# Block attention and FFN in one kernel: transposes and narrow attn*v products placed between the FFN's 512-column products

## Chip, cores and metric

The kernel runs on one core of a Trainium2 chip. The metric is the device time of one execution in microseconds (us); the median of several executions is compared.

## The reference

Two stages, all in float32. First a block-causal attention over q, k, v of shape (8 batches, 8 heads, 576 positions, 64), then a feed-forward network (FFN) on the 4608 tokens with 512 features that come out of it:

```python
scores = scale * np.matmul(q, k.transpose(0, 1, 3, 2))
mask = block_i >= block_j                      # blocks of 64 positions
scores = np.where(mask, scores, -1000000000.0)
scores = scores - np.max(scores, axis=-1, keepdims=True)
attn = np.exp(scores)
attn = attn / (np.sum(attn, axis=-1, keepdims=True) + 1e-09)
...
x = np.ascontiguousarray(attn_out.transpose(0, 2, 1, 3)).reshape(B * S, H * D)
h = x @ w_in                                   # 512 -> 2048
g = np.where(pos, h, np.where(neg, 0.0, (h + beta) ** 2 / (4.0 * beta)))
return (g @ w_out).astype(np.float32)          # 2048 -> 512
```

## The kernel before

**Precision.** Products run on the type float32r. To keep float32's accuracy, an operand is split into a high word and a low word (`hi`, and `lo`, the remainder), and a product is made of two or three partial products.

**Attention.** The work goes by pairs of heads: 8 batches of 4 pairs, 32 pairs (`Pair`, with `b` the batch and `hp` the pair). One pair goes through `scores` (two accumulated products into a PSUM bank, row maximum on VectorE, exp on ScalarE, reciprocal and scaling on VectorE, L497 to L520), three groups of query tiles for each of the two heads (`scores(j, g)`) and the last 64 queries of both heads together (`scores_last`). The probabilities lie with queries on partitions and must be turned: they go through a DMA into a float32r tile (`prr`, L251), and `turn(j, g)` and `turn_last` transpose them on TensorE, 128 columns at a time (L559), into a PSUM bank, from which `split` (L552, L554) writes hi and lo words to the tiles `pa` and `pb`. `attn_v_first` and `attn_v` multiply them with v (`weighted`, L598): products of 320, 256, 192, 128 and 64 columns. `add_words` (L620, L621) adds the two words' sums and `store_x` writes x for the FFN.

**q and k.** For batches 0 and 1 they are split and then transposed. From batch 2 on (`raw`) they are transposed as they are (`turned_raw`, L403, four transposes for a head into one bank; `turned_last`, L444, one transpose for the last blocks) and split by four operations out of PSUM (`parted`, L390, L391, L396, L397). This is done for the next pair while the present one is worked on; `turned_last` is done in the pair itself.

**Batches 2 and later** (`far`) have one more property: a pair's last transpositions and its attn*v run on into the steps of the next pair, in which it is called `old`.

**FFN.** For each of 9 chunks of 512 tokens and each of 16 slices of 128 hidden features, `ffn_in` makes 12 products of 512 columns into the one bank `ph` (L777), the activation and the split follow on ScalarE, VectorE and GpSimd (L786 to L792), and `ffn_out` makes 12 products of 512 columns into the four banks `po` (L801, L806).

**PSUM.** Eight banks: four for `po`, one for `ph`, three "work" banks, which all scores, transpositions and attn*v take in turn (`work_bank`).

**Order of the work.** `attention_steps` is a generator that yields eight times for a pair. After each yield from step 36 on, the loop at the end (L845) emits one block of 12 FFN products. So in the program TensorE gets an attention part, in one piece, then 12 wide products, and so on. A scheduler then orders each engine's instructions; it keeps to the order of the program except where, by its own estimate, an instruction isn't ready and a later one is. In the part with batches 2 and later TensorE's order in the trace is that of the program. One pair of heads is then, on TensorE (T transposes of probabilities, Q transposes of q and k, S scores, A attn*v, F an FFN product; the group or the head in brackets):

```
step 0   T x3 (1,1 of old), S x4 (0,0), A x8 (first, of old), F x12
step 1   T x4 (1,2 of old), S x2 (0,1), Q x1 (last blocks), F x12
step 2   A x10 (head 1 of old), S x2 (0,2), F x12
step 3   T x3 (0,0), S x8 (last queries), F x12
step 4   T x3 (0,1), S x4 (1,0), Q x4 (head 0 of next), F x12
step 5   T x4 (0,2), S x2 (1,1), F x12
step 6   T x5 (last queries), S x2 (1,2), F x12
step 7   T x3 (1,0), A x10 (head 0), Q x4 (head 1 of next), F x12
```

Of the kernel before, what the change touches and what calls it, by code (L numbers as in the profile page):

```python
# [23 lines left out]
def block_attn_then_ffn(  # L24
# [53 lines left out]
    def work_bank(name):  # L78
# [178 lines left out]
    class Pair:  # L257
# [141 lines left out]
        def turned_raw(self, j):  # L399

            ps = work_bank("ps_qk")
            for t in range(NTL):
                nc.tensor.transpose(  # L403
                    ps[:, t * P : (t + 1) * P].bitcast(F32R), self.qk[:, j * NTL + t, :, :], ident_r
                )
            self.parted(
                lambda x: x[:, j, :SM].rearrange("p (c t) -> p c t", t=NTL),
                ps[:, :SM].rearrange("p (t c) -> p c t", t=NTL),
            )
            for a, bt, hi0 in ((qa, qb, 0), (ka, kb, D)):  # L410
                nc.sync.dma_start(
                    a[:D, j, :SM].bitcast(F32), bt[hi0 : hi0 + D, j, :SM].bitcast(F32)
                )

        def turned(self, is_q, j):
# [7 lines left out]
            for t in range(NTL):  # L423
                nc.tensor.transpose(
                    ps[:, t * P : (t + 1) * P].bitcast(F32R), src[:, j * NTL + t, :, :], ident_r
                )

# [11 lines left out]
        def turned_last(self):  # L439

            ps = work_bank("ps_qk")
            if self.raw:
                ps = ps[:, :P]
                nc.tensor.transpose(ps.bitcast(F32R), self.qk[:, 2 * NTL, :, :], ident_r)  # L444
                ps = ps.rearrange("p (h c) -> p h c", h=2)
                self.parted(last_blocks, ps)
                for i, a in enumerate((qa, ka)):
                    nc.vector.tensor_scalar_mul(
                        last_blocks(a)[:D], ps[i * D : (i + 1) * D], 1.0 if i else SCALE
                    )  # L450
                return
            for i, src in enumerate((self.qs, self.ks)):
                nc.tensor.transpose(
                    ps[:, i * P : (i + 1) * P].bitcast(F32R), src[:, 2 * NTL, :, :], ident_r
                )
            for i, (a, bt, hi0) in enumerate(((qa, qb, 0), (ka, kb, D))):
# [26 lines left out]
        def product(self, ps, j, c0, k0, n, first, last):  # L483
            nc.tensor.matmul(  # L484
                ps, qa[:KA, j, c0 : c0 + P], ka[:KA, j, k0 : k0 + n], start=first, stop=False
            )
            nc.tensor.matmul(  # L487
                ps, qb[:, j, c0 : c0 + P], kb[:, j, k0 : k0 + n], start=False, stop=last
            )

# [65 lines left out]
        def transposed(self, out, parts, c0, n):  # L556
            src = parts[c0 // TCH][:, c0 % TCH : c0 % TCH + n] if self.hop else parts[0][:, c0 : c0 + n]
            if self.hop:
                nc.tensor.transpose(out.bitcast(F32R), src, ident_r)  # L559
            else:  # L560
                nc.tensor.transpose(out, src, ident)  # L561

# [31 lines left out]
        def weighted(self, ps, j, parts, first=True, last=True):  # L594
            for i, (kt, lo_col, mov) in enumerate(parts):
                vt = self.vs[j][: (BLK if self.plain and kt == NTL else P), kt, :, :]
                for m, x in enumerate(mov):
                    nc.tensor.matmul(  # L598
                        ps[:, lo_col:], vt, x,
                        start=first and i == 0 and m == 0,  # L600
                        stop=last and i == len(parts) - 1 and m == len(mov) - 1,
                    )

# [66 lines left out]
    def attention_steps():  # L670
# [10 lines left out]
        for i, cur in enumerate(pairs + [None]):  # L681
            nxt = pairs[i + 1] if i + 1 < len(pairs) else None
            far = old is not None and old.far
            near = old is not None and not old.far
            if far:
                old.turn(1, 1)
            if cur:
# [22 lines left out]
            if not cur:  # L710
                return
            if cur.far:
                cur.scores(0, 2)
            else:
                cur.begin()
                cur.scores(0, 2)
                cur.turn(0, 0)
            yield
            if cur.far:
                cur.begin()  # L720
                cur.turn(0, 0)
                cur.scores_last()
            else:
                cur.scores_last()
                cur.turn(0, 1)
            if nxt:
                nxt.load_qk()
                nxt.split_q()
            yield
            if nxt:  # L730
                nxt.split_k()
            if cur.far:
                cur.turn(0, 1)
                cur.scores(1, 0)
            else:
                cur.scores(1, 0)
                cur.turn(0, 2)
            if nxt:
                nxt.turned(True, 0)
            yield  # L740
            if cur.far:
                cur.turn(0, 2)
                cur.scores(1, 1)
            else:
                cur.scores(1, 1)
                cur.turn_last()
            if nxt:
                nxt.turned(False, 0)
            yield
            if cur.far:  # L750
                cur.turn_last()
                cur.scores(1, 2)
            else:
                cur.scores(1, 2)
                cur.attn_v(0)
                cur.turn(1, 0)
            yield
            if cur.far:
                cur.turn(1, 0)
                cur.attn_v(0)  # L760
# [3 lines left out]
            if nxt:  # L764
                nxt.turned(True, 1)
            yield
            old = cur


    def ffn_in(c, fc):  # L770
# [4 lines left out]
        for cc in range(NCC):  # L775
            for i, (w, x) in enumerate(((wih, xh), (wih, xl), (wil, xh))):
                nc.tensor.matmul(  # L777
                    ph, w[:, cc, fs], x[:, cc, xs],
                    start=(cc == 0 and i == 0), stop=(cc == NCC - 1 and i == 2),
                )  # L780

# [15 lines left out]
    def ffn_out(po, c, fc, gh, gl, wo):  # L797
        for tt in range(NTT):
            ts_ = slice(tt * P, (tt + 1) * P)
            for w in range(2):  # L800
                nc.tensor.matmul(  # L801
                    po[tt], gh[:, ts_], wo[:, w, :], start=(fc == 0 and w == 0), stop=False
                )
        for tt in range(NTT):
            ts_ = slice(tt * P, (tt + 1) * P)
            nc.tensor.matmul(po[tt], gl[:, ts_], wo[:, 0, :], start=False, stop=fc == NFC - 1)  # L806
        if fc < NFC - 1:
# [12 lines left out]
    def feed_forward():  # L820
        prev = None
        for c in range(NCH):
            for fc in range(NFC):
                cur = (c, fc, *ffn_in(c, fc))
                yield
                if prev is not None:
                    if prev[1] == 0:
                        po = [ps_o.tile([P, DM], F32, tag="po", name="po") for _ in range(NTT)]
                    ffn_out(po, *prev)
                    yield  # L830
                prev = cur
        ffn_out(po, *prev)
        yield
# [8 lines left out]
    weights = prepare_weights()  # L842
    ffn_steps = feed_forward()
    converted = 0
    for i, _ in enumerate(attention_steps()):  # L845
        if i < START:
# [45 lines left out]
```

## Time and profile before

| What | Value |
|---|---|
| Median of 3 runs | 1240.96 us (1238.43, 1240.97, 1240.96) |
| The profiled execution | 1239.06 us, its span 1237.3 us |
| Mean granted TensorE clock | 0.989 |
| TensorE, weight loads | busy 1186.6 us, 993.1 us; 6280 instructions each |
| VectorE, ScalarE, GpSimd | busy 863.8, 698.5, 371.8 us |
| DMA | 215.40 MB, mean 174 GB/s |

PE stands for TensorE's matmuls and PEld for its weight loads, DVE for VectorE, ACT for ScalarE, POOL for GpSimd, SP for SyncE, which issues the DMAs. The ends of matmuls are modelled, and their recorded intervals overlap, so a busy PE says little about how well it is used. In a row of the timeline the first number is the start and the second the duration, both in us; then follow engine, line, operation, the tile written and those read, and the shape. In a row of the groups by line the numbers behind the bar are busy time in us, mean duration in ns and the idle time of the engine ahead of it.

### The profile page before, as it was taken

To read this page: it belongs to the slowest core of one execution; us is meant where nothing else is said; L and a number is where in the kernel's file an instruction comes from. 1 tells how busy PE (TensorE), PEld (TensorE's weight loads), DVE (VectorE), ACT (ScalarE), POOL (GpSimd) and SP (SyncE) were. 2 spreads that over 40 slices of the span, in tenths; PEclk is the share of its full clock that TensorE was granted. 3 is DMA by queue.
4 is the path that set the end of the run, shared out by engine and by line. 5 is a ranking of instruction groups with operands and counts; after the bars stand their busy time and mean duration, and the time that the engine had idled before them with its cause. 6 is when DMAs were issued, how large, how long until landed. Compare 5 with 4: busy or idle time off the path is not lost.

```text
span 1237.3 us, 19822 instructions
## 1 busy us (share of the span) xinstructions
PE 1186.6 (96%) x6280; PEld 993.1 (80%) x6280; DVE 863.8 (70%) x2124; ACT 698.5 (56%) x1731; POOL 371.8 (30%) x366
## 2 busy tenths in 40 slices
PE   4878898999999999999999999999999999999998
PEld 3666677788888888888888888888888888888886
DVE  8888778658777877787777877787778776322322
ACT  5877667546566656665666665666566654222222
POOL 3444546312222222222222222222222222222222
PEclk9988998999999999999999999999999999999999
DMA  5756776778986655565555555565556443333332
GB/s 165 213 176 208 235 247 221 225 202 255 291 270 219 192 162 156 147 198 166 163 159 180 164 160 160 148 196 151 155 149 192 142 135 111 119 102 102 120 103 102
DMA packets 177192, 215.40 MB, mean 174 GB/s; under 512 B 109872, under 2 KB 128304, under 8 KB 176320
## 3 DMA queue, kind: packets, MB, share of 16 engines
q1 hardware_dynamic: 177088, 214.14, 56.1%
q8 instruction: 50, 0.82, 0.3%
q14 instruction: 54, 0.44, 0.1%
HBM read 134.74 MB, written 31.98 MB: 135 GB/s over the span
## 4 chain that ended last, share of the span: by engine, by line
PE 86%; DVE 5%; DMA 4%; ACT 2%; issue 2%; POOL 1%; SPq 0%; ACTq 0%; DVEq 0%; POOLq 0%
PE ph L777 31%; PE po L801 20%; PE po L806 10%; PE ps_av L598 9%; PE ps_s L484 5%; PE ps_s L487 4%; PE ps_t L559 4%; PE ps_qk L403 1%; DMA bits<-in_moe_w_in_dram 1%; DVE bits L172 1%; POOL bits L184 1%; PE ps_t L561 1%; DVE nm L508 1%; DVE bits L178 1%; DVE shifted L175 1%
## 5 line engine op out<-in xcount | busy, mean ns | idle before, releaser
L792 POOL TENSOR_TENSOR gl<-t,gh 128x512 fp32r<-128x512 f32 x144 | 186.5, 1295 | 522.8 <-ACT gh L791 338.2
L801 PE MATMUL po<-wo,gh 128*128 128x512 f32 x1152 | 294.1, 396 | 0.1
L801 PEld LDWEIGHTS po<-wo,gh 128*128 128x128 f32 x1152 | 211.2, 188 | 43.3 <-ACT gh L791 0.6
L777 PE MATMUL ph<-xh,wih 128*128 128x512 f32 x576 | 232.7, 404 | 0.4 <-DVE t L790 0.4
L777 PE MATMUL ph<-xh,wil 128*128 128x512 f32 x576 | 228.1, 396 | 0.0
L777 PE MATMUL ph<-xl,wih 128*128 128x512 f32 x576 | 226.9, 394 | 0.0
L787 DVE SCALAR_TENSOR_TENSOR t<-t 128x512 f32<-128x512 f32 x144 | 101.0, 701 | 161.5 <-ACT t L786 158.6
L786 ACT ACTIVATE t<-ph 128x512 f32<-128x512 f32 x144 | 86.2, 599 | 160.5 <-PE ph L777 160.5
L791 ACT CAST gh<-t 128x512 fp32r<-128x512 f32 x144 | 89.4, 621 | 118.9 <-DVE t L790 118.8
L806 PE MATMUL po<-wo,gl 128*128 128x512 f32 x576 | 155.3, 391 | 0.0
L484 PE MATMUL ps_s<-ka,qa 68*128 68x288 f32 (+4 forms) x384 | 133.8, 363 | 4.9 <-DMA ka<-mrow 4.0
L513 ACT ACTIVATE pr<-ps_s,nm 128x128 f32<-128x128 f32 x192 | 100.4, 525 | 57.5 <-DVE nm L508 56.4
L508 DVE TENSOR_REDUCE nm<-ps_s 128x1 f32<-128x128 f32 (+3 forms) x256 | 118.9, 482 | 16.4 <-PE ps_s L487 15.6
L777 PEld LDWEIGHTS ph<-xh,wil 128*128 128x128 f32 x576 | 109.1, 189 | 24.0
L806 PEld LDWEIGHTS po<-wo,gl 128*128 128x128 f32 x576 | 108.0, 188 | 22.9
L777 PEld LDWEIGHTS ph<-xl,wih 128*128 128x128 f32 x576 | 109.6, 190 | 19.3
L777 PEld LDWEIGHTS ph<-xh,wih 128*128 128x128 f32 x576 | 109.2, 190 | 19.3 <-DVE t L790 0.8
L381 POOL TENSOR_TENSOR vsr<-vn,vsr 64x64 fp32r<-64x64 f32 (+1 forms) x96 | 56.5, 589 | 227.1 <-ACT vsr L380 226.0
L487 PE MATMUL ps_s<-kb,qb 128*128 128x288 f32 (+4 forms) x384 | 120.4, 321 | 0.0
L790 DVE TENSOR_TENSOR t<-ph,t 128x512 f32<-128x512 f32 x144 | 98.7, 685 | 2.0
L559 PEld LDWEIGHTS ps_t<-ident_r,prr 128*128 128x128 f32 x600 | 68.5, 139 | 22.4 <-issue 0.5
L494 DVE TENSOR_SCALAR sm<-sm 128x1 f32<-128x1 f32 x256 | 38.5, 151 | 65.0 <-ACT pr L513 54.8
(115 smaller groups left out, 1879.7 us busy)
## 6 DMA issues: line engine op xcount, KB each, us to landing
wo<-wo_split SPq DMA_DIRECT2D x144, 512.0 KB, 3.4
prr<-pr SPq DMA_DIRECT2D x96, 192.0 KB, 3.0
prr<-pr SPq DMA_DIRECT2D x48, 256.0 KB, 2.8
out_dram<-ob SPq DMA_DIRECT2D x36, 256.0 KB, 2.9
bits<-in_moe_w_in_dram SPq DMA_DIRECT2D x16, 512.0 KB, 4.6
bits<-in_moe_w_out_dram SPq DMA_DIRECT2D x16, 512.0 KB, 4.0
wo_split<-ws SPq DMA_DIRECT2D x16, 512.0 KB, 2.9
qa<-qb SPq DMA_DIRECT2D x63, 128.0 KB, 2.4
```

Of the source, the lines that this page charges most:

```text
L484: nc.tensor.matmul(ps, qa[:KA, j, c0 : c0 + P], ka[:KA, j, k0 : k0 + n], start=first, stop=False)
L487: nc.tensor.matmul(ps, qb[:, j, c0 : c0 + P], kb[:, j, k0 : k0 + n], start=False, stop=last)
L508: nc.vector.tensor_reduce(out=nm[:, i : i + 1], in_=ps[:, cs], axis=AX.X, op=ALU.max, negate=True)
L513: nc.scalar.activation(raw[:, cs], ps[:, cs], AF.Exp, bias=nm[:, i : i + 1], scale=1.0, accum_out=sm[:, i : i + 1],)
L559: nc.tensor.transpose(out.bitcast(F32R), src, ident_r)
L598: nc.tensor.matmul(ps[:, lo_col:], vt, x, start=first and i == 0 and m == 0, stop=last and i == len(parts) - 1 and m == len(mov) - 1,)
L777: nc.tensor.matmul(ph, w[:, cc, fs], x[:, cc, xs], start=(cc == 0 and i == 0), stop=(cc == NCC - 1 and i == 2),)
L787: nc.vector.scalar_tensor_tensor(out=t_, in0=t_, scalar=1.0, in1=t_, op0=ALU.min, op1=ALU.mult)
L790: nc.vector.tensor_tensor(out=t_, in0=ph, in1=t_, op=ALU.max)
L792: nc.gpsimd.tensor_tensor(out=gl, in0=t_, in1=gh.bitcast(F32), op=ALU.subtract)
L801: nc.tensor.matmul(po[tt], gh[:, ts_], wo[:, w, :], start=(fc == 0 and w == 0), stop=False)
L806: nc.tensor.matmul(po[tt], gl[:, ts_], wo[:, 0, :], start=False, stop=fc == NFC - 1)
```

## The change

An object `feed` now holds the generator of FFN products, and that generator yields after every single product. For each step `feed.open()` makes 12 products available. `feed.tick()` emits one of them; `feed.rest(keep)` emits those that are left, down to `keep`.

- Each transpose of probabilities of a pair of batch 2 or later is followed by one tick; each raw transpose of q and k is preceded by one; each attn*v product of such a pair with at most 128 columns is preceded by one.
- The transpositions of probabilities move from the beginning of a step to the end of the step before, behind a second yield. The first yield of a step hands over how many FFN products to keep for them.
- `scores(0, 2)` comes ahead of the old pair's attn*v in step 2; `begin()`, with the split of v, moves with the first transposition to the end of step 2.
- While the old pair is of batch 2 or later and there is a present one (23 of the 32 pairs), every TensorE instruction of these functions goes through `in_order`, which pins it behind the one that the program emits before it. Nothing is computed differently, and the number of instructions is the same.

One pair, in the same notation, becomes:

```
step 0   S x4, A x2, F A F A, A x2, F A F A, F x4, (T F) x4 (1,2 of old)
step 1   S x2, F Q, F x11
step 2   S x2, A x8, F A F A, F x7, (T F) x3 (0,0)
step 3   S x8, F x9, (T F) x3 (0,1)
step 4   S x4, (F Q) x4, F x4, (T F) x4 (0,2)
step 5   S x2, F x7, (T F) x5 (last queries)
step 6   S x2, F x9, (T F) x3 (1,0)
step 7   A x8, F A F A, (F Q) x4, F x3, (T F) x3 (1,1)
```

The core of the diff; the lines left out wrap further matmuls in `in_order`, add `yield` between the FFN's products, and shift the calls of `attention_steps` as listed above:

```diff
+    class Feed:
+        def __init__(self, products):
+            self.products, self.left, self.pinned = products, 0, False
+        def open(self):
+            self.left = 3 * NCC
+        def tick(self):
+            if self.left:
+                self.left -= 1
+                next(self.products, None)
+        def rest(self, keep=0):
+            while self.left > keep:
+                self.tick()
+    feed = Feed(None)
+    def in_order(ins):
+        return tc.keep_in_program_order(ins) if feed.pinned else ins
...
             for t in range(NTL):
-                nc.tensor.transpose(
+                feed.tick()
+                in_order(nc.tensor.transpose(
                     ps[:, t * P : (t + 1) * P].bitcast(F32R), self.qk[:, j * NTL + t, :, :], ident_r
-                )
+                ))
...
             if self.hop:
-                nc.tensor.transpose(out.bitcast(F32R), src, ident_r)
-            else:
-                nc.tensor.transpose(out, src, ident)
+                in_order(nc.tensor.transpose(out.bitcast(F32R), src, ident_r))
+            else:
+                in_order(nc.tensor.transpose(out, src, ident))
+            if self.far:
+                feed.tick()
...
                 for m, x in enumerate(mov):
-                    nc.tensor.matmul(
+                    if self.far and ps.shape[1] - lo_col <= P:
+                        feed.tick()
+                    in_order(nc.tensor.matmul(
                         ps[:, lo_col:], vt, x,
...
-            if far:
-                old.turn(1, 1)
+            feed.pinned = far and cur is not None
...
-            yield
+            yield NTL if far else 0
             if far:
                 old.turn(1, 2)
+            yield
...
             if far:
+                if cur:
+                    cur.scores(0, 2)
                 old.attn_v(1)
                 old.store_x()
...
+            if cur.far:
+                yield NTL - 1
+                cur.turn(1, 1)
+            else:
+                yield 0
             yield
             old = cur
...
         if i >= START:
             banks["free"] = False
-            next(ffn_steps, None)
-    for _ in ffn_steps:
+            feed.rest(keep)
+        next(steps, None)
+        feed.rest()
+        if i + 1 >= START:
+            feed.open()
+    for _ in feed.products:
         pass
```

More of the change, by code (lines that the diff above doesn't have):

```diff
@@ L731, in attention_steps @@
                 nxt.split_k()
[L732 to L736, printed above, removed]
+            cur.scores(1, 0)
+            if not cur.far:
                 cur.turn(0, 2)
@@ L739, in attention_steps @@
                 nxt.turned(True, 0)
-            yield
[L741 to L745, printed above, removed]
+            if cur.far:
+                yield NTL
+                cur.turn(0, 2)
+            else:
+                yield 0
+            yield
+            cur.scores(1, 1)
+            if not cur.far:
                 cur.turn_last()
@@ L748, in attention_steps @@
                 nxt.turned(False, 0)
+            if cur.far:
+                yield NTL + 1
+                cur.turn_last()
+            else:
+                yield 0
+            yield
+            cur.scores(1, 2)
+            if cur.far:
+                yield NTL - 1
+                cur.turn(1, 0)
+            else:
+                cur.attn_v(0)
+                cur.turn(1, 0)
+                yield 0
             yield
             if cur.far:
[L751 to L759, printed above, removed]
                 cur.attn_v(0)
@@ L765, in attention_steps @@
                 nxt.turned(True, 1)
+            if cur.far:
+                yield NTL - 1
+                cur.turn(1, 1)
+            else:
+                yield 0
             yield
@@ L842, in block_attn_then_ffn @@
     weights = prepare_weights()
-    ffn_steps = feed_forward()
+    feed.products = feed_forward()
     converted = 0
-    for i, _ in enumerate(attention_steps()):
+    steps = attention_steps()
+    for i, keep in enumerate(steps):
         if i < START:
```

63 lines of the change are left out of this document (37 added, 26 removed).

## The prediction

> **What bounds the kernel now.** I read the page first, then the trace by stretches, then TensorE's weight loads in order of time.
>
> ```profile
> span 1237.3 us, 19822 instructions
> PE 1186.6 (96%) x6280; PEld 993.1 (80%) x6280; DVE 863.8 (70%) x2124; ACT 698.5 (56%) x1731; POOL 371.8 (30%) x366
> PEclk9988998999999999999999999999999999999999
> PE 86%; DVE 5%; DMA 4%; ACT 2%; issue 2%; POOL 1%; SPq 0%; ACTq 0%; DVEq 0%; POOLq 0%
> 300.00:1000.00 700.00, 699.02 (x3891) 594.64 (x3890) 546.19 (x1378) 431.22 (x1110) 192.48 (x202) 1.00 0.59 179
> ```
>
> TensorE holds 86% of the chain that ended last. The last row is the window 300 to 1000 us (busy PE, PEld, DVE, ACT, POOL, then clock): TensorE is busy for 699.02 of 700 us at full clock, VectorE for 546. But a matmul's recorded interval overlaps the next one's, so a stall between two of them hardly shows there. The weight loads (PEld) are the better clock: in an unbroken stream the load of the next product begins when the present product begins to stream, as these rows show (start, duration, engine, line, tile):
>
> ```profile
> 600.13 0.19 PEld L777 LDWEIGHTS ph<-xl,wih 128*128 128x128 f32 x1
> 600.36 0.19 PEld L777 LDWEIGHTS ph<-xh,wil 128*128 128x128 f32 x1
> 600.59 0.19 PEld L777 LDWEIGHTS ph<-xh,wih 128*128 128x128 f32 x1
> ...
> 245.01 0.11 PEld L559 LDWEIGHTS ps_t<-ident_r,pre 128*64 128x64 f32 x1
> 245.18 0.19 PEld L777 LDWEIGHTS ph<-xh,wil 128*128 128x128 f32 x1
> 245.29 0.19 PEld L777 LDWEIGHTS ph<-xh,wih 128*128 128x128 f32 x1
> ...
> 1046.82 0.54 PEld L559 LDWEIGHTS ps_t<-ident_r,prr 128*128 128x128 f32 x4
> 1047.30 0.19 PEld L777 LDWEIGHTS ph<-xh,wih 128*128 128x128 f32 x1
> 1047.41 0.19 PEld L777 LDWEIGHTS ph<-xl,wih 128*128 128x128 f32 x1
> ```
>
> The 512-column product takes 0.23 us (600.13, 600.36, 600.59); its successor's weights are loaded well within that. At 245 us one transpose stands alone between two 512-column products, which is the arrangement the change wants everywhere. The wide product's weights begin to load at 245.18, when the transpose begins, and the next load at 245.29, when the wide product begins: the lone transpose holds TensorE for 0.11 us, though it has only 128 columns to stream (a quarter of 0.23 is 0.06). So only one load is made ahead, and the narrow product's time is the load of what follows it. At 1046.82 four transposes stand in a row. The first begins 0.23 later, at 1047.05; the fourth begins at 1047.30 with the wide product's load; the wide product begins at 1047.41. That is (1047.30 - 1047.05)/3 = 0.083 us for a transpose followed by a transpose, and 0.11 for the last. A transpose's successor that is itself a transpose loads faster than a wide product does. This decides the first term below.
>
> **What a head pair costs now.** Here is the one transpose of the last blocks (L444) in two pairs, and what it waits for:
>
> ```profile
> 590.66 0.14 PEld L444 LDWEIGHTS ps_qk<-ident_r,qk 128*128 128x128 f32 x1 [0.35 <-PE ps_s L487]
> ...
> 622.77 0.43 DVE L621 TENSOR_TENSOR x<-ps_av,xtmp 64x256 f32<-64x256 f32 x1
> 622.77 0.19 PEld L487 LDWEIGHTS ps_s<-kb,qb 128*128 128x128 f32 x1
> 623.31 0.14 PEld L444 LDWEIGHTS ps_qk<-ident_r,qk 128*128 128x128 f32 x1 [0.35 <-PE ps_s L487]
> ```
>
> A pair takes 623.31 - 590.66 = 32.65 us. L621, the last reader of the attn*v bank three allocations back, ends at 622.77 + 0.43 = 623.20, and the load follows at 623.31: the work banks rotate over three, a bank comes free 0.11 after its last reader, and this wait costs about 0.37 us a pair (0.54 to the next load, where a 384-column product should take some 0.17, which is 0.23 x 384/512).
>
> **The change, part by part.** The instructions are the same; only TensorE's order changes, and with it when banks, DMA targets and the other engines' inputs are due. Counts, from the groups by line:
>
> ```profile
> L559 PE MATMUL ps_t<-ident_r,prr 128*128 128x128 f32 x576 | 68.5, 235 | 0.1
> L403 PE MATMUL ps_qk<-ident_r,qk 128*128 128x128 f32 x192 | 23.7, 247 | 0.0
> L444 PE MATMUL ps_qk<-ident_r,qk 128*128 128x128 f32 x24 | 5.9, 244 | 0.9
> L598 PE MATMUL ps_av<-pa,vsr 128*128 128x128 f32 x96 | 16.1, 250 | 0.0
> L598 PE MATMUL ps_av<-pcs,vsr 128*128 128x64 f32 x96 | 15.7, 246 | 0.0
> L559 PE MATMUL ps_t<-ident_r,prr 128*64 128x128 f32 x24 | 5.4, 224 | 0.0
> ```
>
> Over the 24 pairs of batches 2 to 7 that is 25 attention transposes a pair, 9 of q and k, 4 + 4 narrow attn*v products. Of these pairs 23 run with the order pinned.
>
> *(a) Lone narrow products.* The 25 transposes stand in 7 runs now (3, 3, 4, 5, 3, 3, 4), so 18 are followed by a transpose at 0.083; the 9 stand in runs of 4, 4 and 1, so 6 are. In the seventh step the last narrow attn*v product is also followed by a transpose. All 25 will be followed by a wide product at 0.11: 25 x 0.025 = +0.62 us a pair. The other narrow attn*v products are followed by an ordinary load either way: nothing. Bounds: -1.6 (rival 2) to +0.7.
> The Trainium skill, TensorE: Matmul & The Clock Gate, section LDWEIGHTS, puts a weight load at its columns over 1.2, 107 ns for 128, whatever is loaded. The lone transpose's 0.11 agrees, the run's 0.083 does not, and the measurement decides; by the rule alone this term would be nothing and the sum some 14 us lower.
>
> *(b) A new wait for a bank.* In the last step of a pair the four transposes of q and k (L403) fill a bank, and two allocations lie between it and the next pair's first attn*v (256 columns). Its readers are a chain over ScalarE and VectorE:
>
> ```profile
> 615.11 0.19 PEld L777 LDWEIGHTS ph<-xh,wih 128*128 128x128 f32 x1
> 615.21 0.19 PEld L777 LDWEIGHTS ph<-xl,wih 128*128 128x128 f32 x1
> 615.57 0.59 ACT L390 ACTIVATE qb<-ps_qk 64x512 fp32r<-64x512 f32 x1
> 616.20 0.68 DVE L391 SCALAR_TENSOR_TENSOR qb<-ps_qk,qb 64x512 fp32r<-64x512 f32 x1 [0.21 <-ACT qb L390]
> 616.91 0.58 ACT L396 CAST kb<-ps_qk 64x512 fp32r<-64x512 f32 x1 [0.75 <-DVE qb L391]
> 617.53 0.69 DVE L397 TENSOR_TENSOR kb<-ps_qk,kb 64x512 fp32r<-64x512 f32 x1 [0.65 <-ACT kb L396]
> ...
> 618.26 0.19 PEld L487 LDWEIGHTS ps_s<-kb,qb 128*128 128x128 f32 x1
> ...
> 618.61 1.01 PEld L598 LDWEIGHTS ps_av<-pa,vsr 128*128 128x128 f32 x8
> 619.53 1.69 PEld L801 LDWEIGHTS po<-wo,gh 128*128 128x128 f32 x8
> ```
>
> The last transpose ends at 615.21, the four readers, each waiting for the one before, at 618.22: 3.01 us. Now twelve wide products cover that and the load for attn*v starts at 618.61, 0.39 late enough. After the change the four transposes have swallowed four of the twelve. What is left behind the last: three wide products 0.68, three times transpose and wide product 3 x (0.11 + 0.23) = 1.02, and the scores' products up to the load, 618.61 - 618.26 = 0.35. That is 2.05 against 3.01 + 0.11: a wait of 1.07 us, with everything on TensorE queued behind it. The bank in between, that of the moved third transposes, is filled later and could be no earlier. Bounds: 0 (if the slots fall differently) to 1.6 (where the readers queue behind other work by a further half, as the next item's do).
>
> *(c) The wait of L444.* The bank's first attn*v ends at 619.53 + 0.11, its last reader at 623.20, 3.56 later. After the change 4 wide products, 4 transposes with theirs, two 384-column products and one wide product lie between: 0.91 + 1.36 + 0.34 + 0.23 = 2.84. If its readers hung on attn*v alone, the wait would grow from 0.37 to 0.8. But what they queue behind is the softmax of the scores just before, and the wait of (b) and four wide products now lie between those scores and the end of attn*v, so the softmax is done sooner relative to it; four readers of about 0.4 each (L621 has 0.43) fit into 2.84. I take -0.37, and keep +0.45 as the other end.
>
> *(d) What else moves, at nothing.* Each transposition of probabilities comes up to a half step earlier. They read what SP's queue brings; the nearest is this one:
>
> ```profile
> 607.30 0.48 SPq L251 DMA_DIRECT2D prr<-pr  x1
> ...
> 613.03 0.46 PEld L559 LDWEIGHTS ps_t<-ident_r,prr 128*128 128x128 f32 x3
> ...
> prr<-pr SPq DMA_DIRECT2D x96, 192.0 KB, 3.0
> ```
>
> It lands about 610.8 with its issue (607.30 + 0.48 + 3.0) and is read at 613.03: 2.2 us of room, of which at most three transposes with their wide products, 1.0, are used up. The splits of v on ScalarE and GpSimd, which are emitted earlier too, and the loads of q, k and v behind SP's waits have no consumer within a step. If that cover is gone, a late landing costs its own lateness. The swap of scores(0, 2) with attn*v moves a bank's need by less than 1.5 us, with 12 wide products around it.
>
> **Sum.** 0.62 + 1.07 - 0.37 = +1.3 us a pair, times 23 pairs = 30 us. On the profiled execution, 1237.3 us of span and 1239.06 in all, that gives 1269; the median of the runs, 1240.96, lies 1.9 above it. I say 1270.
>
> **Rivals.**
> 1. *Price without the new wait.* (a) stays, the bank for attn*v is handed out otherwise or freed in time. With (c) as it is: 23 x 0.62 = 14, 1253; with the wait of L444 gone as well, 23 x 0.25 = 6, 1245. For it: the 0.39 of room now, and that the other engines' order is not pinned and can adapt. Against: 3.01 us is four operations back to back.
> 2. *Faster: the loads hide.* If behind a wide product TensorE loaded both the narrow product's weights and those of the next wide one, each of the 34 transposes would cost 0.06 instead of 24 x 0.083 + 10 x 0.11 = 3.1 us together, and the 8 narrow attn*v 0.4 instead of 0.9: -1.5 us a pair, 1239 - 35 = 1204. The point that decides is whether a load may start before the narrow product does. Against: at 245.18 it starts with it.
> The Trainium skill, same page, section on the array as 16 sub-arrays, says that TensorE's queue is a partial reorder window that can pull weight loads ahead of matmuls in flight, which taken for more than one load is this rival; the rows show one load ahead, no more.
> 3. *Slower still.* (b) at 1.07 and (c) at +0.45: 2.14 x 23 = 49, 1288, and more where further banks come late, since a pinned order cannot step around any of them.
> 4. *No difference.* The pinned order would have to equal today's, or relief equal price: (a) 0.62 against at most 0.37 of wait.
>
> **How the numbers follow.** Forecast (1256 to 1280) 0.56; rival 1 (1243 to 1256) 0.22; rival 3 (1280 to 1305) 0.12; rival 2 0.05, and 0.01 for another gain; no difference 0.04. The range 1243 to 1288 takes in the forecast, rival 1 and the nearer half of rival 3. Slower by over 0.2% (2.5 us, about what a measurement can tell from no change) 0.90, within 0.04, faster 0.06.
>
> **What would show it.** In the changed kernel: behind each transpose between wide products, two loads 0.11 apart; a gap of about a microsecond in front of the first 256-column attn*v of each pair, ended by L397's counterpart; the wait at L444's counterpart gone; a pair of about 34 us. Wrong would be: lone transposes at 0.06, no gap at attn*v, or other transposes waiting for DMA landings.

## The result, and the profile after

The changed kernel takes 1274.32 us (median; 1273.36 to 1275.14), the kernel before 1240.5. The ratio is 1.0276, with a 95% interval of 1.0258 to 1.0293: slower by 2.8%. The forecast was 1270. The profiled execution took 1275.14 us, its span 1273.4, which is 36.1 more than before.

The page of the changed kernel, with the rows that answer to those shown of before (busy time, the chain that ended last):

```profile
span 1273.4 us, 19858 instructions
PE 1204.3 (95%) x6280; PEld 991.7 (78%) x6280; DVE 863.1 (68%) x2124; ACT 698.8 (55%) x1731; POOL 367.5 (29%) x366
PE 80%; DVE 7%; ACT 5%; DMA 3%; issue 2%; POOL 1%; SPq 0%; ACTq 0%; DVEq 0%; POOLq 0%
```

TensorE, VectorE, ScalarE and GpSimd run as many counted instructions as before; the 36 more in all (19858 against 19822) are semaphore instructions, so "the number of instructions is the same", said of the change, holds for the work alone. The other engines are about as busy as before, and the mean granted clock is 0.986 against 0.989. But in the chain TensorE has lost 6 points, and VectorE and ScalarE have gained 5: it now waits for them.

The first place is the one that the prediction named. These are the end of one pair and the beginning of the next, in the changed kernel's timeline (weight loads and the last reader of the bank of the q and k transposes):

```profile
598.18 0.19 PEld L825 LDWEIGHTS ph<-xl,wih 128*128 128x128 f32 x1
...
598.32 0.59 ACT L413 ACTIVATE qb<-ps_qk 64x512 fp32r<-64x512 f32 x1 [0.83 <-PE ps_qk L427]
...
599.92 0.19 PEld L512 LDWEIGHTS ps_s<-kb,qb 128*128 128x128 f32 x1
...
600.14 0.19 PEld L512 LDWEIGHTS ps_s<-kb,qb 128*128 128x128 f32 x1
...
600.28 0.69 DVE L420 TENSOR_TENSOR kb<-ps_qk,kb 64x512 fp32r<-64x512 f32 x1 [0.65 <-ACT kb L419]
...
601.09 0.30 PEld L627 LDWEIGHTS ps_av<-pa,vsr 128*128 128x128 f32 x2 [0.76 <-PE ps_s L512]
```

The last transpose ends at 598.18, L420 at 600.28 + 0.69 = 600.97, and 0.12 later, at 601.09, the load for the first attn*v begins. The load before it began at 600.14; 0.12 would have been its time (0.23 x 256/512), so TensorE stands for 0.83 us. The readers took 2.79 where 3.01 was forecast, because the first of them started sooner.

The second place is the transpose of the last blocks, here in two pairs that follow one another:

```profile
571.87 0.14 PEld L469 LDWEIGHTS ps_qk<-ident_r,qk 128*128 128x128 f32 x1
...
605.51 0.19 PEld L825 LDWEIGHTS ph<-xh,wih 128*128 128x128 f32 x1
605.83 0.14 PEld L469 LDWEIGHTS ps_qk<-ident_r,qk 128*128 128x128 f32 x1
```

A pair takes 33.96 us instead of 32.65. The wait at this transpose is 605.83 - 605.51 - 0.17 = 0.15 us instead of 0.37.

The third place was not forecast: once in four pairs, where one chunk of the FFN ends, in the middle of a pair. First TensorE's loads, then ScalarE's operations beside them, then VectorE's:

```profile
417.24 0.14 PEld L584 LDWEIGHTS ps_t<-ident_r,prr 128*128 128x128 f32 x1
417.45 0.19 PEld L825 LDWEIGHTS ph<-xh,wil 128*128 128x128 f32 x1
417.58 0.14 PEld L584 LDWEIGHTS ps_t<-ident_r,prr 128*128 128x128 f32 x1
...
417.93 0.14 PEld L584 LDWEIGHTS ps_t<-ident_r,prr 128*128 128x128 f32 x1
...
418.48 0.19 PEld L825 LDWEIGHTS ph<-xh,wil 128*128 128x128 f32 x1
420.09 0.19 PEld L509 LDWEIGHTS ps_s<-ka,qa 68*128 68x128 f32 x1 [1.43 <-ACT pr L538]
```

```profile
418.40 0.59 ACT L577 CAST pb<-ps_t 128x512 fp32r<-128x512 f32 x1 [1.75 <-PE ps_t L584]
418.88 0.59 ACT L867 COPY ob<-po 128x512 f32<-128x512 f32 x1
419.35 0.60 ACT L538 ACTIVATE pr<-ps_s,nm 128x384 f32<-128x384 f32 x1
```

```profile
417.27 0.68 DVE L869 COPY ob<-po 128x512 f32<-128x512 f32 x1
417.87 0.55 DVE L533 TENSOR_REDUCE nm<-ps_s 128x1 f32<-128x384 f32 x1
```

The copies out of the `po` banks (L867, L869) and the split of the turned probabilities (L577, which waits 1.75 us for the interleaved transposes) stand ahead of a softmax (L533, L538) in the two engines' order. Its bank comes free at 419.95, and the pinned scores(1, 2) wait until 420.09 with everything behind them: 1.5 us. Such a pair takes 434.56 - 399.19 = 35.37 us:

```profile
399.19 0.14 PEld L469 LDWEIGHTS ps_qk<-ident_r,qk 128*128 128x128 f32 x1
...
434.56 0.14 PEld L469 LDWEIGHTS ps_qk<-ident_r,qk 128*128 128x128 f32 x1
```

The first of these fences also shows the price of a transpose that stands alone. From its load at 417.24 to that of the next at 417.58 and 417.93 it is 0.34 and 0.35 us for a transpose and a wide product; less 0.227 for the wide product (the median, in both traces between 430 and 940 us, of those that stand between two others), that is about 0.117 for the transpose, against 0.083 in a row.

### The profile page after: what moved, and what is told of

It is laid out like the page before. It is cut to its first block, busy times and chain, and to the rows that moved or that the text cites. A ratio compares the mean times of both kernels' runs of the same rounds, so it can differ in the third digit from the quotient of the medians.

```text
span 1273.4 us, 19858 instructions
## 1 busy us (share of the span) xinstructions
PE 1204.3 (95%) x6280; PEld 991.7 (78%) x6280; DVE 863.1 (68%) x2124; ACT 698.8 (55%) x1731; POOL 367.5 (29%) x366
## 4 chain that ended last, share of the span: by engine, by line
PE 80%; DVE 7%; ACT 5%; DMA 3%; issue 2%; POOL 1%; SPq 0%; ACTq 0%; DVEq 0%; POOLq 0%
PE ph L825 28%; PE po L851 20%; PE po L857 11%; PE ps_av L627 8%; PE ps_s L509 4%; PE ps_s L512 3%; PE ps_t L584 3%; DVE kb L420 1%; DVE qb L414 1%; ACT qb L413 1%; ACT kb L419 1%; PE ps_qk L427 1%; DMA bits<-in_moe_w_in_dram 1%; PE ps_t L586 1%; DVE nm L533 1%
## 5 line engine op out<-in xcount | busy, mean ns | idle before, releaser
L851 PE MATMUL po<-wo,gh 128*128 128x512 f32 x1152 | 319.1, 405 | 1.2 <-DVE pr L544 1.0
L825 PE MATMUL ph<-xl,wih 128*128 128x512 f32 x576 | 235.8, 409 | 0.0
L825 PE MATMUL ph<-xh,wil 128*128 128x512 f32 x576 | 234.8, 408 | 0.0
L857 PE MATMUL po<-wo,gl 128*128 128x512 f32 x576 | 191.3, 424 | 0.0
L404 POOL TENSOR_TENSOR vsr<-vn,vsr 64x64 fp32r<-64x64 f32 (+1 forms) x96 | 50.6, 528 | 299.3 <-ACT vsr L403 297.8
L538 ACT ACTIVATE pr<-ps_s,nm 128x128 f32<-128x128 f32 x192 | 100.4, 525 | 62.2 <-DVE nm L533 60.9
L584 PE MATMUL ps_t<-ident_r,prr 128*128 128x128 f32 x600 | 133.0, 222 | 0.1
L533 DVE TENSOR_REDUCE nm<-ps_s 128x1 f32<-128x128 f32 (+3 forms) x256 | 120.7, 482 | 15.3 <-PE ps_s L512 13.8
L509 PE MATMUL ps_s<-ka,qa 68*128 68x288 f32 (+4 forms) x384 | 121.6, 332 | 9.9 <-ACT pr L538 5.5
L584 PEld LDWEIGHTS ps_t<-ident_r,prr 128*128 128x128 f32 x600 | 83.0, 138 | 7.6 <-DVE t L840 0.5
```

The lines of the kernel that those rows point to most:

```text
L509: in_order(nc.tensor.matmul(ps, qa[:KA, j, c0 : c0 + P], ka[:KA, j, k0 : k0 + n], start=first, stop=False))
L533: nc.vector.tensor_reduce(out=nm[:, i : i + 1], in_=ps[:, cs], axis=AX.X, op=ALU.max, negate=True)
L538: nc.scalar.activation(raw[:, cs], ps[:, cs], AF.Exp, bias=nm[:, i : i + 1], scale=1.0, accum_out=sm[:, i : i + 1],)
L584: in_order(nc.tensor.transpose(out.bitcast(F32R), src, ident_r))
L825: in_order(nc.tensor.matmul(ph, w[:, cc, fs], x[:, cc, xs], start=(cc == 0 and i == 0), stop=(cc == NCC - 1 and i == 2),))
L851: in_order(nc.tensor.matmul(po[tt], gh[:, ts_], wo[:, w, :], start=(fc == 0 and w == 0), stop=False))
```

## The experiments

**The theory.** Three terms: (1) a transpose alone costs more than one in a row; (2) a bank that must be read out before it is filled again, with fewer wide products left to cover the reading; (3) the wait at the chunk's end, from the pinned order. **The rivals:** the pinning or the earlier place of the transpositions is what costs; or the lone price explains all; or, for (2), the waits don't belong to single banks, but ScalarE and VectorE bound the whole stretch.

### How much of it is the interleaving

*No FFN product between narrow ones; order, place and pinning as in the changed kernel.*

```diff
         def tick(self):
-            if self.left:
-                self.left -= 1
-                next(self.products, None)
+            pass
         def rest(self, keep=0):
             while self.left > keep:
-                self.tick()
+                self.left -= 1
+                next(self.products, None)
```

> The changed order with its pinning and its moved transpositions, but no FFN product between narrow products: they stand in runs again, now at the end of a step. Theory (price of lone narrow products 0.6 us a pair, wait for the bank of the q and k transposes 0.83 us a pair, both from the interleaving, 1.3 us at each chunk boundary from the pinned order): runs restore 0.083 us for a transpose, nine wide products follow the last transpose of q and k, so both terms go; about 1241, at most 1246 if a boundary wait stays. Rival A (pinning or the earlier place of the transpositions is what costs, the interleaving nothing): 1268 to 1275.

Measured: 1243.62 us, ratio 1.0031 (1.0017 to 1.0045). Rival A falls: pinning and the earlier transpositions together cost 3 us, the interleaving, with the waits that it brings, the rest. A pair takes 32.74 us:

```profile
561.71 0.14 PEld L468 LDWEIGHTS ps_qk<-ident_r,qk 128*128 128x128 f32 x1 [0.23 <-PE po L856]
594.45 0.14 PEld L468 LDWEIGHTS ps_qk<-ident_r,qk 128*128 128x128 f32 x1 [0.24 <-PE po L856]
```

*Only the transposes of probabilities interleaved.* The ticks ahead of the raw transposes and of the narrow attn*v are taken out.

```diff
-                feed.tick()
                 in_order(nc.tensor.transpose(
                     ps[:, t * P : (t + 1) * P].bitcast(F32R), self.qk[:, j * NTL + t, :, :], ident_r
...
-                    if self.far and ps.shape[1] - lo_col <= P:
-                        feed.tick()
```

> The changed kernel with FFN products only between the transposes of probabilities; the raw transposes of q and k and the narrow attn*v products stand in runs. Theory: 18 x 0.025 = 0.45 us a pair remain of the lone price, no wait at the first attn*v (9 wide products 2.04, three transposes with theirs 1.02 and scores 0.35 make 3.41 against 3.12), wait of the last-blocks transpose 0.1 instead of 0.37, boundary waits stay: 23 x 0.25 + 6 x 1.1 = +12, about 1253. Rival B (the whole loss is the price of lone narrow products, 33 us over 42 x 23 of them, 0.034 each): 25 of the 42 remain, 1240.5 + 20 = 1260, with no wait at attn*v in either kernel.

Measured: 1254.35, ratio 1.011 (1.0089 to 1.013). The theory's figure; rival B's 1260 is outside the interval. The pair takes 33.11 us, 0.37 more than with nothing interleaved, where 18 x 0.025 = 0.45 was expected. That is net of waits: the kernel with nothing interleaved waits 0.06 longer at the transpose of the last blocks (0.23 against 0.17) and 0.19 us at one scores product of each pair (its load at 577.53), where this one doesn't. The lone price itself is then some 0.6, and the nearness of 0.37 to 0.45 is in part luck:

```profile
563.39 0.14 PEld L467 LDWEIGHTS ps_qk<-ident_r,qk 128*128 128x128 f32 x1 [0.17 <-PE po L853]
596.50 0.14 PEld L467 LDWEIGHTS ps_qk<-ident_r,qk 128*128 128x128 f32 x1 [0.17 <-PE po L853]
```

*The reverse: only the raw transposes and the narrow attn*v interleaved.*

```diff
                 in_order(nc.tensor.transpose(out, src, ident))
-            if self.far:
-                feed.tick()
```

> The changed kernel with the transposes of probabilities in runs again; FFN products only between the raw transposes of q and k and the narrow attn*v. Theory: the lone price falls by 18 x 0.024 = 0.43 us a pair, the wait at the first attn*v stays, since three wide products, a run of three, three wide products and scores make 2.0 us against 2.9: 0.8 us; boundary waits at 0.6 to 1.3: 1240.5 + 23 x 0.8 + 5 = 1264. Rival (the waits come from the interleaved transposes of probabilities, which keep their banks open longer): 1247, with no wait at attn*v.

Measured: 1276.99, ratio 1.0303 (1.0288 to 1.0318): a miss for both theories. With fewer lone transposes the kernel isn't faster but as slow as the changed one. Of the wait at the first attn*v 0.2 us is left, but the transpose of the last blocks now waits 1.2 us in each pair, longer than at this place in any other run. First its load, then VectorE beside it:

```profile
572.88 0.14 PEld L469 LDWEIGHTS ps_qk<-ident_r,qk 128*128 128x128 f32 x1 [1.20 <-DVE pb L579]
```

```profile
572.15 0.68 DVE L579 TENSOR_TENSOR pb<-ps_t,pb 128x512 fp32r<-128x512 f32 x1
572.86 0.43 DVE L648 TENSOR_TENSOR x<-ps_av,xtmp 64x256 f32<-64x256 f32 x1
```

The load follows the end of L579, 572.83, the split of the group turned just before, and the transpose is over when the load after next begins, at 573.07. L648, the last reader of the attn*v bank, ends only at 573.29. So here the transpose doesn't take that bank. The description of the kernel before says that the work banks are taken in turn; this run shows that it isn't always so: when the readers' order changes, another bank can be the one that is free. So waits cannot be added up term by term.

### Whose wait is it

*The four transposes of q and k ahead of attn*v in step 7*, so that their bank has attn*v's time more to be read out.

```diff
-            if cur.far:
+            if cur.far and nxt:
+                nxt.turned(True, 1)
+            if cur.far:
                 cur.attn_v(0)
...
-            if nxt:
+            if nxt and not cur.far:
                 nxt.turned(True, 1)
```

> The changed kernel with one swap: in step 7 the four interleaved transposes of q and k stand ahead of attn*v of head 0 instead of behind it, so that their bank has some 1.7 us more to be read out. As many lone products as in the changed kernel. Theory: the gap of 0.83 us at the first 256-column attn*v goes, 23 x 0.83 = 19 less, 1255. Rival B: nothing changes, 1274.

Measured: 1273.12, ratio 1.0253 (1.0234 to 1.0272): a miss. The gap that should go is gone, and nearly as long a one has come up at the transpose of the last blocks. First TensorE's loads at the two places, then ScalarE's second copy of the two words' sums, then the last reader of the bank that this transpose takes:

```profile
600.74 0.19 PEld L512 LDWEIGHTS ps_s<-kb,qb 128*128 128x128 f32 x1
...
600.97 0.19 PEld L512 LDWEIGHTS ps_s<-kb,qb 128*128 128x128 f32 x1
601.09 0.31 PEld L627 LDWEIGHTS ps_av<-pa,vsr 128*128 128x128 f32 x2
...
605.52 0.19 PEld L827 LDWEIGHTS ph<-xh,wih 128*128 128x128 f32 x1
606.50 0.14 PEld L469 LDWEIGHTS ps_qk<-ident_r,qk 128*128 128x128 f32 x1 [0.79 <-PE ph L827]
```

```profile
605.50 0.36 ACT L649 COPY xtmp<-ps_av 64x256 f32<-64x256 f32 x1 [0.48 <-DVE x L650]
```

```profile
605.96 0.43 DVE L650 TENSOR_TENSOR x<-ps_av,xtmp 64x256 f32<-64x256 f32 x1
```

The load at 601.09 follows at once; that at 606.50 comes 0.98 after the one before it, where 0.17 would do: 0.81 us.

*The changed kernel without the pinning* (`feed.pinned = False`).

> The changed kernel without the pinning: same program, but the scheduler may move TensorE's instructions. Its order differs in two places only: three wide products are pulled ahead of the first 256-column attn*v of each pair, and at chunk boundaries six are pulled ahead of the scores(1, 2). The transposes stay alone between wide products. Theory: 0.68 of the 0.83 us of bank wait a pair and 1.1 us of each boundary wait are covered: 1274 - 23 x 0.68 - 6 x 1.1 = 1252; what is left above 1240.5 is the lone price, 14, less what the last-blocks wait gained. Rival B: 1274, since the lone products are unchanged.

Measured: 1276.27, ratio 1.0283 (1.0266 to 1.0301): a miss again. The order did change as described, and the 0.83 us ahead of attn*v are filled with three wide products. But new waits stand elsewhere, 0.4 us each in front of scores and of the transpose of the last blocks, and a regular pair takes 34.4 us instead of 34.0. At the chunk's end the forecast came true: six wide products are pulled ahead of the scores(1, 2), whose load at 421.08 has only 0.16 us of idle time before it, and such a pair takes 34.5 us, about as long as the others. The new waits outweigh that (loads first, then L650):

```profile
600.08 0.19 PEld L512 LDWEIGHTS ps_s<-kb,qb 128*128 128x128 f32 x1
...
600.43 0.55 PEld L851 LDWEIGHTS po<-wo,gh 128*128 128x128 f32 x3
601.25 0.88 PEld L627 LDWEIGHTS ps_av<-pa,vsr 128*128 128x128 f32 x7 [0.28 <-issue]
...
605.09 0.19 PEld L509 LDWEIGHTS ps_s<-ka,qa 68*128 68x128 f32 x1 [0.42 <-ACT pr L538]
...
606.00 0.14 PEld L469 LDWEIGHTS ps_qk<-ident_r,qk 128*128 128x128 f32 x1 [0.44 <-PE ph L825]
```

```profile
605.46 0.43 DVE L650 TENSOR_TENSOR x<-ps_av,xtmp 64x256 f32<-64x256 f32 x1
```

These two runs and the changed kernel have one thing in common. Take as zero the end of the last product into `ph`, that is, the beginning of the first scores product (the load of the second): 599.92 in the changed kernel, 600.74 with q and k first, 600.08 unpinned. From there to the end of L650, the last reader of the bank, it is

```profile
605.29 0.43 DVE L650 TENSOR_TENSOR x<-ps_av,xtmp 64x256 f32<-64x256 f32 x1
```

605.72 - 599.92 = 5.80 us in the changed kernel, 606.39 - 600.74 = 5.65 with q and k first, 605.89 - 600.08 = 5.81 unpinned, and the transpose of the last blocks loads 0.11 later in all three. TensorE's own work in this stretch, loads to loads without the waits, is nearly the same before and after: 623.31 - 617.98 - 0.37 = 4.96 and 605.83 - 599.92 - 0.83 - 0.15 = 4.93.

In the kernel before the last product into `ph` begins with the load at 617.75, of the next one's weights, and ends 0.23 later, at 617.98; from there the readers take 623.20 - 617.98 = 5.22. Two of ScalarE's operations show most of the difference, the first copy of the two words' sums (L620, after the change L649) and the exp of the softmax (L513, L538); TensorE's load first, then before, then after:

```profile
617.75 0.46 PEld L559 LDWEIGHTS ps_t<-ident_r,prr 128*128 128x128 f32 x3
```

```profile
619.85 0.37 ACT L620 COPY xtmp<-ps_av 64x256 f32<-64x256 f32 x1
...
621.43 0.37 ACT L513 ACTIVATE pr<-ps_s,nm 128x128 f32<-128x128 f32 x1
```

```profile
603.56 0.37 ACT L649 COPY xtmp<-ps_av 64x256 f32<-64x256 f32 x1
603.96 0.37 ACT L538 ACTIVATE pr<-ps_s,nm 128x128 f32<-128x128 f32 x1
```

The exp begins 621.43 - 617.98 = 3.45 after the zero before, 603.96 - 599.92 = 4.04 after it in the changed kernel: 0.59 later, as much as the whole chain is longer. Before, ScalarE makes the copy at a time at which it would wait for VectorE's part of the FFN's activation; now attn*v comes later, and the copy stands directly ahead of the exp, 0.40 us. The other 0.19 comes from the split of q and k: ScalarE (L419, to 600.25) and VectorE (L420, to 600.97) are still at it when the FFN's activation is due.

With q and k first neither holds, and the exp begins 2.98 after the zero; but both sums now stand behind the softmax, and the second copy waits 0.48 us for the first sum. So 5.80 and 5.65 are two different chains, and no rule seen here makes them equal. The length isn't a constant of the stretch: L650's counterpart ends 4.82 after the beginning of the first scores product in the run without interleaving, and 6.7 after it in the reverse run (L648). What the three kernels show is that the readers' chain, and not a single bank, sets when TensorE gets on, and that an order of TensorE changes the readers' order with it. That is read from the rows; no run changed the readers' order alone.

*Both moves: q and k first, and the transpose of the last blocks at the beginning of step 2*, out of the stretch.

```diff
                 cur.scores(0, 1)
-                cur.turned_last()
+                if not cur.far:
+                    cur.turned_last()
...
             yield
+            if cur and cur.far:
+                cur.turned_last()
             if far:
```

> The changed kernel with both moves: transposes of q and k ahead of attn*v in step 7, and the transpose of the last blocks at the beginning of step 2. In the run with the first move alone the wait moved from the first attn*v (0.83 to 0) to this transpose (0.15 to 0.81). Theory 1 (two banks, two dues; giving both more room ends both): 23 x 0.9 less than the changed kernel, about 1253. Theory 2 (ScalarE and VectorE together bound the stretch, whoever is next waits): 1268 to 1274, with a new wait at the scores or elsewhere. The lone price and the boundary waits stay under both.

Measured: 1257.57, ratio 1.0145 (1.0123 to 1.0167). Neither figure, but far nearer to the first: 17 of the 21 us, and both waits are gone (the first attn*v loads at 592.64, 0.12 after the load before it, and the transpose has no idle time ahead); the pair takes 33.20 us:

```profile
566.79 0.14 PEld L469 LDWEIGHTS ps_qk<-ident_r,qk 128*128 128x128 f32 x1
...
599.99 0.14 PEld L469 LDWEIGHTS ps_qk<-ident_r,qk 128*128 128x128 f32 x1
```

So inside the stretch the wait moved on, as theory 2 has it, and it went, as theory 1 has it, once the bank that ends the stretch was asked for later.

*On top of it, the transposes of probabilities in runs again* (the edit of the reverse run above): the lone price with few waits in the kernel that it starts from.

> The changed kernel with both moves, which had nearly no bank waits left (pairs of 33.2 us, 1257.6 us in all), and with the transposes of probabilities in runs again: the lone price by itself, without waits on top. Theory: 18 x 0.024 = 0.43 us a pair less, 23 x 0.43 = 10, 1248, with pairs of 32.8. Rival (lone or in a row, a transpose costs the same, as a load time of 107 ns for 128 columns would have it): 1257.

Measured: 1251.01, ratio 1.0093 (1.0072 to 1.0115), 6.6 us less; the rival (no difference) falls, the size is two thirds of that expected. The pair takes 32.93, 0.27 less. But TensorE now waits at three scores products of a regular pair, 0.2 to 0.3 us each, where the run with both moves waits at the chunk's end alone, so the 0.27 is the lone price less these waits:

```profile
564.13 0.14 PEld L469 LDWEIGHTS ps_qk<-ident_r,qk 128*128 128x128 f32 x1
597.06 0.14 PEld L469 LDWEIGHTS ps_qk<-ident_r,qk 128*128 128x128 f32 x1
```

### The wait at the chunk's end

```diff
-        if fc < NFC - 1:
+        if fc < NFC - 1 or c < NCH - 1:
             return
```

> The changed kernel without the copies and output DMAs of the first eight chunks (so only the last chunk's output is written). Theory (at a chunk boundary the copies out of the FFN's four output banks stand ahead of a softmax in ScalarE's and VectorE's order, its bank is late, and the pinned scores(1, 2) wait 1.5 us for it): the pairs of 35.34 us become pairs of 34.0, 6 x 1.34 = 8 less, 1266; the waits of the other pairs stay. Rival (the boundary's wait comes from the order alone, not from the copies): 1273.

Measured: 1268.58, ratio 1.0235 (1.0213 to 1.0256). The pair at the chunk's end takes 34.05 us like every other, instead of 35.37. The edit takes out the output DMAs with the copies; that it is the copies is what the rows at 417 us show. Nor is the pair longer in the run without the pinning. So it takes both, the copies ahead of the softmax and a pinned order that cannot step around the wait:

```profile
401.71 0.14 PEld L469 LDWEIGHTS ps_qk<-ident_r,qk 128*128 128x128 f32 x1
435.76 0.14 PEld L469 LDWEIGHTS ps_qk<-ident_r,qk 128*128 128x128 f32 x1
```

### A version that beats both

What is left to gain in the kernel before is the 0.37 us at the transpose of the last blocks. *First by twelve products:* it is emitted at the beginning of step 2, the second half of the edit above, in the kernel before.

> The kernel before, with the transpose of the last blocks (L444) emitted at the beginning of step 2 instead of the end of the scores in step 1, twelve wide products later. Theory 1 (each wait belongs to its bank): its wait of 0.31 us a pair on average goes and none comes, since the bank's readers end long before; 1240.5 - 23 x 0.31 = 1233. Theory 2 (the stretch is bounded by the readers' chain, and the next one in line waits instead): no gain, 1240.

Measured: 1252.88, ratio 1.0111 (1.0096 to 1.0126): slower, a miss for both theories. With the transpose its six readers moved, the order on ScalarE and VectorE changed, and new waits came up, here at the scores(1, 1) of step 5:

```profile
580.25 0.19 PEld L484 LDWEIGHTS ps_s<-ka,qa 68*128 68x128 f32 x1 [0.55 <-ACT pr L513]
```

*Then by two, and by four products.* The FFN's generator yields after each product, as in the change, and from batch 2 on two (four) of step 1's twelve are emitted ahead of the transpose:

```diff
                 cur.scores(0, 1)
+                if cur.far:
+                    some(2)
                 cur.turned_last()
...
-            next(ffn_steps, None)
+            some(3 * NCC - feed["ahead"])
+            feed["ahead"] = 0
```

> The kernel before with one transpose moved: from batch 2 on, the transpose of the last blocks (L444) is emitted behind the first two FFN products of step 1 instead of ahead of all twelve. The other engines' orders stay word for word as they were (in the run with twelve products ahead they changed, and waits came up elsewhere). Theory: the two products, 0.45 us, cover its wait of 0.37 us, the readers' chain is as long as before and ends under work; lone or not it costs 0.11; 22 x 0.31 = 7 less, 1233. Rival (whoever is next in the stretch waits instead): 1240.

> The same with four FFN products ahead. ScalarE's and VectorE's orders change in two places a pair. Theory: nothing is left to cover, so 1233 again; if the changed order of the readers costs, 1236 to 1245, with a wait at scores.

Measured: 1235.03, ratio 0.9960 (0.9946 to 0.9974), and 1234.15, ratio 0.9965 (0.9952 to 0.9978), both faster than the kernel before. With two products ahead the pair takes 32.44 us instead of 32.65, and there is no idle time at the load:

```profile
590.69 0.14 PEld L451 LDWEIGHTS ps_qk<-ident_r,qk 128*128 128x128 f32 x1
...
623.13 0.14 PEld L451 LDWEIGHTS ps_qk<-ident_r,qk 128*128 128x128 f32 x1
```

The gain is 0.4%, about two thirds of the 7 us expected: a regular pair gains 0.25 us (32.70 to 32.45, the medians), the pair at the chunk's end almost nothing.

## Why the prediction was right

**What bounds the kernel.** Right. Reading the weight loads as the clock gave the figures on which the rest stands.

**(a) Lone narrow products, +0.62 us a pair.** Right in kind. Measured by what remains: of a regular pair's growth, 33.96 - 32.65 = 1.31, the bank wait takes 0.83 and the wait at the last blocks gives back 0.22, which leaves 0.70. (By the prediction's own 0.11 and 0.083 the term would be 25 x 0.027 = 0.67.) The rows at 417 us make a lone transpose 0.117 us, a little over the 0.11 read from one case before; by these rows the term would be 25 x 0.034 = 0.85. The runs that switch the transposes of probabilities between alone and in a row give 0.37 and 0.27 a pair, net of the waits that come or go with it; with these, the first gives some 0.6 for the 18 alone, and 18 x 0.034 is 0.61. So the term was sized somewhat too small.

**(b) The new wait, +1.07.** Right in place and cause, 0.83 in size: the readers' chain was read from a pair in which it started 0.36 us after the last transpose; it now starts 0.14 after it (598.32 against 598.18). That the wait is this bank's is shown by the run with q and k first, in which it is gone.

**(c) The wait at the last blocks, -0.37.** It fell to 0.15. The prediction let this relief lean on the wait of (b), which gives the softmax time, and that held: the run with q and k first took (b) away, and (c) rose to 0.81, the end that the prediction had kept as a bound (0.8). What was wrong is that rival 1 takes (b) away and leaves (c) at 0.37 or less, as if the two were separate. The two hang on one chain of readers, which ends 5.8 us after the end of `ph`, and the change made that chain 0.6 longer, which the prediction did not look for.

**(d) What else moves, at nothing.** This step failed at one place. It looked at landings and at a bank's need inside a regular pair, not at the pair in which the FFN's output banks are copied out. Such a pair is 35.37 - 33.96 = 1.4 us longer than the others, five times (the waits at 418, 556, 693, 830 and 968 us). In the kernel before it is longer too, by 0.25 (426.88 - 393.94 = 32.94, against a median of 32.70), so that some 1.1 us is the change's.

**Sum.** 23 x 1.31 = 30 for the pairs, as forecast (23 x 1.3 = 30), and 5 x 1.1 = 6 that were missing: 36, against 36.1 measured in the spans. That the sum for a pair came out so nearly, 1.31 against 1.32, is luck: (b) was 0.24 too large, (a) 0.08 and the relief of (c) 0.15 off the other way, and the three cancel.

**The rivals.** No lone transpose at 0.06 us was seen, so rival 2 falls by the same rows. Rival 1, the price without the wait, is what both moves came near to, 1257.57 against its 1245 to 1253, which don't hold the 6 us of the chunk's ends. Rival 3's bound for (c) was reached, but only when (b) was taken away.

**What stays open.** Why the readers' chain is 0.6 us longer than before is read from the rows of ScalarE and VectorE, but not shown by a run: their order was not varied by itself. Nor is the difference between 0.11 and 0.117 for a lone transpose settled.

## What to carry to other kernels

Putting a narrow product between wide ones hid its own weight load here but exposed the wide one's behind it (0.11 us for a transpose): read the time from one weight load to the next, for the narrow product alone and in a row, before interleaving. With few PSUM banks, count what TensorE still has to do between filling a bank and needing it again against what the readers need, and follow that sum over the whole stretch, with the order in which the readers will then stand: here a wait that was removed at one bank came back at the next, until the last one in the stretch was asked for later. Move one instruction by as little as covers its wait, and compare the other engines' orders: two products ahead, which left those orders as they were, gained 4 us, twelve lost 13.

## What the runs showed of the hardware

A transpose between wide products did not cost the 0.11 us seen once before the change but 0.117, and its load and that of the wide product are spaced unevenly (0.21 and 0.13 us, rows at 417 us), so that only their sum can be read.
